# Swapped halves of x, another order of one block's loads and transposes, and two later steps in block 2

## The chip, the cores and the metric

The kernel runs on one core of a Trainium2 chip. The metric is the device time of one execution in microseconds (us), here the median over several runs; beside it stands one execution taken with the hardware profiler.

The profile knows these engines: PE (TensorE matrix multiplications), PEld (its weight loads, which overlap with PE), DVE (VectorE), ACT (ScalarE), POOL (GpSimd) and SP (SyncE, which here only issues DMAs). Each engine works through its own instruction list strictly in the written order and waits at an instruction until what it needs is there. A row "SPq" is an instruction that issues a DMA from SP's list; the transfer itself is over later.

## The reference

Attention inside chunks of 64 rows, then a feed-forward layer with a squared ReLU. With 8 batches, 8 heads, 576 rows and 64 values per head:

```
scores = q_c @ k_c.T / sqrt(64)                 # per chunk of 64 rows
attn   = exp(scores - max) / (sum + 1e-9)
x      = (attn @ v_c) as [4608, 512]            # heads side by side
h      = relu(x @ w_in)                         # w_in: 512 x 2048
out    = (h * h) @ w_out                        # w_out: 2048 x 512
```

## The kernel before, in words

**Groups and blocks.** The 4608 rows are cut into 18 groups of 256 rows (four chunks). Two groups make a block, so there are nine blocks, 0 to 8; block j holds the groups 2j and 2j+1. Groups 14 and 15 (block 7) collect the last chunk of each batch; all other groups are "whole", four chunks in a row of one batch.

**The steps of a group.** Its q, k and v are loaded (`qk_pieces`, `v_pieces`; SP issues them). `cast_qk` (step C) turns q and k into bf16, `transpose_qk_dma` (step TD) transposes them with one DMA on SP's list. `scores` (SC) makes the scores on PE and their exponentials on ACT. `values` (AV, or in two halves AV0 and AV1) multiplies with v on PE and divides on DVE (`out_of_x`, lines 431 and 432), which gives x. `transpose_x` (XT) brings x into the transposed tile xT of its block: up to group 11 on PE (line 526) with a copy on ACT (line 531), from group 12 on as one DMA on SP's list (line 521). A DMA that waits for x or for a cast holds up everything behind it in SP's list.

**PSUM banks of attention.** Up to block 3, SC, each half of AV and each XT take the next of two alternating banks (`att_bank`); a step can start to write only when the one two before it has been read out, by DVE for AV and by ACT for SC and XT.

**The feed-forward of blocks 0 to 3.** `ffn_in` has 16 slots, one for each 128 columns of w_in; PE multiplies, ACT makes the ReLU (line 576) and DVE or ACT the square (lines 583, 581). From block 1 on the second product runs as seven products of half size (`ffn_out`), whose operands are sums of pieces of g, made on DVE (`g_sum`, line 599 with outputs in `w_st`). In block 2 the sums are issued in slots 14 and 15, slots 16 to 18 issue nothing on PE, and the products begin with slot 19. A plan by slot says after which slot the steps of the next block's attention are issued.

**The feed-forward of blocks 4 to 8.** Here the first product is split as well. A block is cut into four steps of w_in (Q, 20 in all), each with seven small products (`quad_step`: A1, B2, A6, C5, A7, C3, A4). Four of them take sums of quarters of xT that DVE makes in `x_sums`: e1, e2, e3 and e4. A quarter is `xs(j, dh, th)`, where `th` says which half of the block's rows it is. In order of use:

```
(e1, xs(j, 0, 1), xs(j, 1, 1), ALU.subtract),
(e2, e1, xs(j, 0, 0), ALU.add),
(e3, e2, xs(j, 1, 0), ALU.subtract),
(e4, xs(j, 0, 1), xs(j, 0, 0), ALU.add)
```

So e1, with which A1 opens a block, and B2, which follows, read only the half `th` = 1; A6 waits for e2, C5 for e3, and these read half 0 too. The steps A7, C3 and A4 of one Q are issued between A1, B2 and A6 of the next, and the seven products of the block before (`ffn_out`) stand between them.

**The order of the work.** The order on every engine is written out by hand: `run` goes through the ticks, one tick for a Q, four slots each, 16 slots to a block; a plan tells which attention steps, loads, casts, transposes and sums are issued in which slot, half slots included. During block j the attention of block j+1 runs and q, k and v of block j+2 are loaded. All loads, TD, and XT from group 12 on are in SP's one list in that order. Output tiles are stored by DMAs of POOL, which also makes some squares and the casts (those of groups 8 and 9 are made by ACT).

Of the kernel before, what the change touches and what calls it, by code (L numbers as in the profile page):

```python
# [144 lines left out]
def kernel(  # L145
# [22 lines left out]
    blocks = [[g, g + 1] for g in range(0, n_grp, 2)]  # L168
    n_blk = len(blocks)
# [7 lines left out]
    def is_whole(g):  # L177
        return chunks[g][0][0] == chunks[g][3][0]
# [5 lines left out]
    QUADS = 4  # L184
# [101 lines left out]
    for g in range(n_grp):  # L286
        if is_whole(g):
# [3 lines left out]
            b, s = chunks[g][0]  # L291
# [23 lines left out]
    def go(pieces):  # L315
        for f in pieces:
            f()
# [21 lines left out]
    state = {}  # L339
    banks = {}  # L340

    def x_tile(j):
        if j not in xTs:
            xTs[j] = att_pool.tile([128, BT // 128, n_dt, 128], BF16, name="xT", bufs=2)
        return xTs[j]

    def att_bank():
        if "out" in banks:
            return ps_att.tile([128, 1024], FP32, name="ps_att")
        state["att"] = state.get("att", 0) + 1  # L350
        if state["att"] % 2:
            return ps_att.tile([128, 1024], FP32, name="ps_att")
        return ps_att2.tile([128, 1024], FP32, name="ps_att2")
# [162 lines left out]

    def transpose_x(g):
        x = state.pop(("x", g))
        dst = x_tile(g // 2)[:, g % 2 * 2:g % 2 * 2 + 2].rearrange("p t h q -> p (t h) q")
        if g >= FIRST_DMA_X:  # L520
            nc.sync.dma_start_transpose(out=dst, in_=x.rearrange("p t h a d -> p (t h a d)"))
            return
        psb = att_bank().bitcast(BF16)[:, 0:1024].rearrange("p (b q) -> p b q", q=128)
        for t in range(2):
            for hp in range(n_hp):
                nc.tensor.transpose(  # L526
                    out=psb[:, t * n_hp + hp, :],
                    in_=x[:, t, hp].rearrange("p a d -> p (a d)"),
                    identity=ident)
        copy = nc.vector.tensor_copy if g == blocks[1][0] else nc.scalar.copy  # L530
        copy(out=dst, in_=psb)  # L531
# [5 lines left out]
    for j in range(n_blk):  # L537
        if j < QUADS:
            at = {(th, fh, h): 4 * th + 2 * fh + h
                  for th in range(2) for fh in range(2) for h in range(2)}  # L540
        else:
# [6 lines left out]
            at = {(*key, 0): s for key, s in zip(keys, old)}  # L548
# [164 lines left out]
    def ffn_out(j):  # L713
# [62 lines left out]
            return kept_sb[state["kept"] % 2]  # L776

        def store(dma, o_sb, half, col, t=None):
            g = blocks[j][half]
            b, s0 = chunks[g][0]  # L780
            t0 = b * S + s0
            if not is_whole(g):

                for p in range(2):
                    dma.dma_start(
                        out=out.rearrange("(b s) d -> s b d", s=S)[
                            s0:s0 + CH, b + p:b + 4:2, col:col + HD],
                        in_=o_sb[p * CH:(p + 1) * CH].rearrange("p (t d) -> p t d", d=HD))
            elif t is None:
                dma.dma_start(  # L790
                    out=out[t0:t0 + GT, col:col + HD].rearrange("(t p) d -> p t d", p=128),
                    in_=o_sb.rearrange("p (t d) -> p t d", d=HD))
            else:
                dma.dma_start(
                    out=out[t0 + t * 128:t0 + (t + 1) * 128, col:col + HD],
                    in_=o_sb[:, t * HD:(t + 1) * HD])
# [112 lines left out]
    SC, AV, XT = scores, values, transpose_x  # L909
    TD = transpose_qk_dma  # L910
# [67 lines left out]
    for j in range(QUADS):  # L978
        grps, nxt, far = blocks[j], blocks[j + 1], blocks[j + 2]
        plan = {}  # L980

        def at(slot, f, *x):
            plan.setdefault(slot, []).append((f, x))

        if j == 0:
            loads, go_slots = pieces(far), range(17)
            at(28, summed(b11_p_b21, b11, b21))
            for slot, f in ((24, TA), (27, SC), (29, AV), (31, XT)):
                at(slot, f, nxt[0])
            at(31, TQ, nxt[1])  # L990
            at(31, summed(b22_m_b21, b22, b21, ALU.subtract))
            phases = [first_ffn_in, ffn_out_by_ft(0)]
        elif j == 1:
            loads, go_slots = itertools.chain(*map(qk_pieces, far)), range(26, 48)
            for slot, f in ((1, TK), (4, SC), (7, AV), (12, XT)):
                at(slot, f, grps[1])
            for i, g in enumerate(nxt):
                for slot, f in ((16 + 4 * i, C), (21 + 4 * i, TD), (36 + i, SC), (38 + 2 * i, AV),
                                (41 + 2 * i, XT)):
                    at(slot, f, g)  # L1000
            for i, g in enumerate(far):
                at(36 + 4 * i, C, g)
                at(42 + 3 * i, TD, g)
            at(2, summed(b12_p_b21, b12, b21))
            at(12, summed(b11_m_b12, b11, b12, ALU.subtract))
            at(20, summed(b12_p_b22, b12, b22))
            out_j = ffn_out(1)
            for i in (20, 27, 29, 31):
                at(i, lambda: next(out_j)())
            phases = [ffn_in(1, [(0, 256, FT_ORDER), (256, 256, FT_ORDER)]), out_j]  # L1010
        else:
            out_j = ffn_out(j)
            for i in (14, 15):
                at(i, lambda: next(out_j)())
            phases = [ffn_in(j, [(0, BT, range(n_ft))])]
            if j == 2:
                loads, go_slots = itertools.chain(*map(v_pieces, nxt), pieces(far)), [
                    *range(16), *range(27, 36)]
                slots = {SC: (6, 9), AV: (11, 14), XT: (14, 17), C: (21, 26), TD: (25, 29)}
                for f in (C, TD):  # L1020
                    for i, g in enumerate(far):
                        at(slots[f][i], f, g)
                phases.append(out_j)
            else:
                loads, go_slots = pieces(far), range(11)
                for f, slots in ((C, (11, 13)), (TD, (13, 15))):
                    for i, g in enumerate(far):
                        at(slots[i], f, g)
                slots = {SC: (2, 4), AV: (7, 10), XT: (13, 15)}
            for f in (SC, AV, XT):  # L1030
                for i, g in enumerate(nxt):
                    at(slots[f][i], f, g)
            if j == 2:
                for i, f in enumerate((summed(a21_p_a22, a21, a22),
                                       summed(a12_m_a21, a12, a21, ALU.subtract),
                                       summed(a11_p_a21, a11, a21))):
                    at(1 + 2 * i, f)
        slot = 0
        for phase in phases:
            for _ in phase:  # L1040
                if slot in go_slots:
                    for f in loads:
                        f()
                        break
                for f, x in plan.get(slot, []):
                    f(*x)
                slot += 1
        assert all(x < slot for x in plan), (j, slot, sorted(plan))
        if j < QUADS - 1:
            go(loads)  # L1050
# [19 lines left out]
    for j in range(QUADS, n_blk):  # L1070
        if j == QUADS:
            n = 14 - LEAD
            slots = [1 + 19 * i // n for i in range(n)]
            assert len(slots) == n
        else:
            slots = [s for s in range(4, 20) if s % 16 not in NO_OUT]
# [20 lines left out]
        if j + 1 < n_blk:  # L1097
            S0, V0, V1, X0 = ((1.5, 3.5), (4.5, 7.5), (6, 9.5), (8.5, 11.5)) if j == QUADS else (
                (0.5, 7), (2, 8), (3.5, 9.5), (3.5, 10)) if is_whole(blocks[j + 1][0]) else (
                (3.5, 9), (5, 10), (7, 11.5), (11.5, 12))  # L1100
            for i, g in enumerate(blocks[j + 1]):
                at(j, S0[i], SC, g)
                at(j, V0[i], AV0, g)
                at(j, V1[i], AV1, g)
                at(j, X0[i], XT, g)
            if j + 2 == n_blk:
                at(j, 22, check_sums)
                at(j, 25.5, count_bad)
            for i, s in enumerate((13.5, 15, 17.5, 18)):
                at(j, s, x_sums, j + 1, i)  # L1110
# [3 lines left out]
            assert next(loads, None) is None  # L1114
        if j + 2 < n_blk:
            more = pieces(blocks[j + 2])
            for s in range(0, 16):
                at(j, s, load, 1 if is_whole(blocks[j + 2][0]) else 2, more)
            for i in range(2):
                at(j, (9, 13)[i], C, blocks[j + 2][i])  # L1120
                at(j, (12, 13.5)[i], TD, blocks[j + 2][i])
    tail = ffn_out(n_blk - 1)
    at(n_blk, 3, lambda: next(tail)())

# [63 lines left out]
```

## Time and profile before

| | |
|---|---|
| median of 3 runs | 288.05 us (287.52 to 288.37) |
| the profiled execution | 287.81 us, of which the profile's span is 286.0 us |
| PE busy | 269.3 us, 94% of the span |
| DVE, ACT, POOL busy | 70%, 58%, 32% |
| DMA bytes | 55.61 MB, mean 194 GB/s |

The profiled execution lies 0.24 us under the median. Rows of the timeline give the start in us from the span's start, how long, engine, line, operation, output and input tiles, and the count; a bracket at the end is the idle time of the engine just before, and what ended it. Equal instructions next to each other are merged into one row. The tile `qk_st` holds the staged q and k, but in the second half of the kernel also the sums e1 to e4 and some pieces of g. The weight sums live in `w_st`, `w_out_sum` and `qk_st`.

### The profile page before, as it was taken

What the parts mean: (1) busy time and instruction counts of PE and PEld (TensorE: products, weight loads), DVE (VectorE), ACT (ScalarE), POOL (GpSimd) and SP (SyncE); (2) the same over time, 40 slices, a digit from 0 to 9 for tenths busy, and PEclk for the clock granted to TensorE, in tenths of its full rate; (3) what the DMA queues carried; (4) which work ended last, traced back from release to release, by engine and by line L of the source; (5) the groups of instructions that cost most, each with busy time, mean ns of one, the idle gap of its engine ahead of it and who ended that gap; (6) DMA issues with size and microseconds to landing.
All of it is one profiled execution on the core that took longest, in us unless ns stands there. A gap on an engine that the chain in (4) does not pass through costs nothing.

```text
span 286.0 us, 7983 instructions
## 1 busy us (share of the span) xinstructions
PE 269.3 (94%) x3291; PEld 205.6 (72%) x3291; DVE 199.1 (70%) x367; ACT 166.0 (58%) x296; POOL 91.8 (32%) x123
## 2 busy tenths in 40 slices
PE   2999999999999799999999999999969999999994
PEld 2774445788764478447879888888847888888783
DVE  1276515999537671599989997789638877994841
ACT  1537614894458664875778666575626654766320
POOL 2047733240450001141245344522612322431612
PEclk9999999999999999999999999999988999999998
DMA  7999999989999976999998997798997320220313
GB/s 220 241 312 388 389 307 274 328 196 168 300 190 232 239 149 145 279 239 189 227 236 175 218 218 182 145 220 193 267 175 170 76 70 6 87 62 7 94 55 112
DMA packets 135480, 55.61 MB, mean 194 GB/s; under 512 B 104272, under 2 KB 131152, under 8 KB 135440
## 3 DMA queue, kind: packets, MB, share of 16 engines
q1 hardware_dynamic: 132432, 45.76, 69.3%
q0 software_dynamic: 2864, 9.18, 9.8%
q8 instruction: 27, 0.44, 0.6%
q10 hardware_dynamic: 144, 0.13, 0.1%
q14 instruction: 13, 0.11, 0.1%
HBM read 36.70 MB, written 9.44 MB: 161 GB/s over the span
## 4 chain that ended last, share of the span: by engine, by line
PE 81%; DVE 7%; DMA 4%; ACT 3%; SPq 3%; issue 1%; ACTq 0%
PE ps_ffn L642 20%; PE ps_out L761 19%; PE ps_ffn L565 15%; PE ps_ffn L761 13%; PE ps_ffn L877 5%; DMA qk_st<-in_k_dram 3%; DVE gT L583 2%; PE ps_att L470 2%; PE ps_att L497 2%; DVE x L432 2%; SPq L279 2%; PE ps_ffn L422 1%; PE ps_att L526 1%; DVE w_st L599 1%; PE ps_ffn L389 1%
## 5 line engine op out<-in xcount | busy, mean ns | idle before, releaser
L565 PE MATMUL ps_ffn<-xT,w_in_bf 128*128 128x512 bf16 (+1 forms) x328 | 58.7, 333 | 0.4 <-DVE xT L531 0.2
L761 PEld LDWEIGHTS <-w_st 128*128 128x128 bf16 x512 | 49.1, 98 | 8.3 <-DVE w_st L599 1.6
L650 DVE CUSTOM_DVE_ANT_0 relu<-ps_ffn,w_st 128x512 f32<-128x512 f32 x60 | 39.4, 684 | 14.5 <-PE ps_ffn L642 13.1
L583 DVE TENSOR_TENSOR gT<-relu 128x256 bf16<-128x256 bf16 (+2 forms) x69 | 33.7, 516 | 20.3 <-ACT relu L576 19.9
L576 ACT ACTIVATE relu<-ps_ffn 128x256 bf16<-128x256 f32 (+2 forms) x82 | 39.9, 503 | 11.7 <-PE ps_ffn L565 10.1
L565 PEld LDWEIGHTS <-w_in_bf 128*128 128x128 bf16 x328 | 30.9, 98 | 21.6 <-DVE xT L531 0.4
L642 PE MATMUL ps_ffn<-qk_st,w_in_bf 128*128 128x256 bf16 x240 | 35.3, 273 | 2.8 <-DVE qk_st L599 2.8
L790 POOL DMA_DIRECT2D out_dram<-o_sb x27 | 19.8, 733 | 53.1 <-DVE o_sb L599 52.0
L642 PEld LDWEIGHTS <-w_in_bf 128*128 128x128 bf16 x320 | 30.8, 98 | 7.3 <-DVE qk_st L599 3.1
L761 PE MATMUL ps_out<-w_out_bf,w_st 128*128 128x256 bf16 x240 | 31.0, 273 | 0.4 <-DVE w_st L599 0.4
L761 PEld LDWEIGHTS <-gT 128*128 128x128 bf16 x296 | 28.6, 98 | 3.4
L684 ACT ACTIVATE w_st<-ps_ffn 128x512 f32<-128x512 f32 x20 | 11.9, 597 | 25.8 <-PE ps_ffn L642 25.8
L481 ACT ACTIVATE e<-ps_att 128x1024 bf16<-128x1024 f32 x18 | 18.4, 1024 | 13.4 <-PE ps_att L470 13.4
L432 DVE TENSOR_TENSOR x<-ps_att,recs 128x512 bf16<-128x512 f32 x36 | 24.9, 691 | 1.2
L642 PEld LDWEIGHTS <-qk_st 128*128 128x128 bf16 x240 | 22.8, 99 | 3.1
L642 PE MATMUL ps_ffn<-xT,qk_st 128*128 128x256 bf16 x160 | 24.4, 277 | 0.0
L661 POOL TENSOR_TENSOR qk_st<-relu 128x512 bf16<-128x512 f32 x10 | 10.3, 1034 | 41.7 <-DVE relu L650 41.7
L661 POOL TENSOR_TENSOR gT<-relu 128x512 bf16<-128x512 f32 x10 | 10.3, 1034 | 41.4 <-DVE relu L650 37.6
L761 PE MATMUL ps_ffn<-w_out_bf,w_st 128*128 128x256 bf16 x144 | 17.6, 273 | 0.3 <-DVE w_st L599 0.3
L659 ACT ACTIVATE gT<-relu 128x512 bf16<-128x512 f32 x28 | 17.7, 633 | 0.0
L438 POOL CAST qkb<-qk_st 128x1024 bf16<-128x1024 f32 x12 | 12.6, 1048 | 15.0 <-DMA qk_st<-in_q_dram 15.0
L599 DVE TENSOR_TENSOR w_st<-gT,w_st 128x1024 bf16<-128x1024 bf16 x26 | 17.3, 700 | 0.0
(91 smaller groups left out, 430.8 us busy)
## 6 DMA issues: line engine op xcount, KB each, us to landing
qk_st<-in_q_dram SPq DMA_DIRECT2D x16, 512.0 KB, 5.4
out_dram<-o_sb POOLq DMA_DIRECT2D x31, 256.0 KB, 4.1
qk_st<-in_k_dram SPq DMA_DIRECT2D x24, 256.0 KB, 5.6
ve_sb<-in_v_dram SPq DMA_DIRECT2D x32, 128.0 KB, 4.0
w_st<-in_moe_w_in_dram SPq DMA_DIRECT2D x8, 512.0 KB, 6.5
w_st<-in_moe_w_out_dram SPq DMA_DIRECT2D x8, 512.0 KB, 5.5
vo_sb<-in_v_dram SPq DMA_DIRECT2D x24, 128.0 KB, 3.4
qk_st<-in_k_dram SPq DMA_DIRECT2D x4, 512.0 KB, 5.9
```

What stands on the lines that cost most here:

```text
L432: nc.vector.tensor_tensor(out=x, in0=o[:, :, :, 0:D], in1=rec.to_broadcast([128, 2, n, D]), op=ALU.mult)
L481: nc.scalar.activation(out=e_out, in_=s_in, func=AF.Exp, scale=scale)
L565: nc.tensor.matmul(out=h[:, 0:n], lhsT=w_in_bf[:, dt, ft * 128:(ft + 1) * 128], rhs=xT[:, c // 128:(c + n) // 128, dt, :], start=(dt == 0) ...
L576: nc.scalar.activation(out=rl[:, 0:n], in_=h[:, 0:n], func=AF.Relu)
L583: nc.vector.tensor_tensor(out=dst, in0=src, in1=src, op=ALU.mult)
L599: nc.vector.tensor_tensor(out=out, in0=in0, in1=in1, op=op)
L642: nc.tensor.matmul(out=bank[:, f * GT:(f + 1) * GT], lhsT=a[:, dt, ft * 128:(ft + 1) * 128], rhs=b[:, :, dt, :], start=(first and f == 0 a ...
L650: nc.vector._custom_dve(TENSOR_ADD_SAT, out=out, in0=in0, in1=in1, s0=BIG, s1=0.0)
L659: engine.activation(out=dst, in_=r, func=AF.Square)
L661: engine.tensor_tensor(out=dst, in0=r, in1=r, op=ALU.mult)
L761: nc.tensor.matmul(out=out_ps, lhsT=lhsT, rhs=b[:, i, :], start=(first and i == 0 and (last or t == 0)), stop=(i == HF - 1), skip_group_ch ...
L790: dma.dma_start(out=out[t0:t0 + GT, col:col + HD].rearrange("(t p) d -> p t d", p=128), in_=o_sb.rearrange("p (t d) -> p t d", d=HD))
```

## The change

Four edits, none of which adds or removes an instruction:

- **Halves.** From block 4 on the even group of a block goes into half 1 of xT and the odd group into half 0 (`half_of`); the stores find the group that belongs to a half accordingly.
- **Block 2's attention steps** (for block 3): AV of group 7 is issued in slot 15 and no longer in 14; XT of group 7 in slot 24 and no longer in 17.
- **XT of group 14** (during block 6): in slot 7.5 and no longer in 11.5.
- **Block 6's loads** (of block 8, groups 16 and 17): the six loads of q and k stay one per slot in slots 0 to 5. The nine loads of v move from slots 6 to 14 to slots 10 (two), 12.5 (three) and 14 to 15.5 (four). TD of group 16 goes from slot 12 to 9.5. XT of group 15 (slot 12) and TD of group 17 (13.5) stay.

In SP's list of block 6 the order after the six loads of q and k was: six loads of v, XT 14, XT 15, one load of v, TD 16, one load of v, TD 17, the last load of v. It becomes: XT 14, TD 16, two loads of v, XT 15, three loads of v, TD 17, four loads of v.

```diff
+    def half_of(g):
+        return g % 2 if g // 2 < QUADS else 1 - g % 2
...
     def transpose_x(g):
         x = state.pop(("x", g))
-        dst = x_tile(g // 2)[:, g % 2 * 2:g % 2 * 2 + 2].rearrange("p t h q -> p (t h) q")
+        n = 2 * half_of(g)
+        dst = x_tile(g // 2)[:, n:n + 2].rearrange("p t h q -> p (t h) q")
...
         def store(dma, o_sb, half, col, t=None):
-            g = blocks[j][half]
+            g, = (g for g in blocks[j] if half_of(g) == half)
...
             if j == 2:
-                slots = {SC: (6, 9), AV: (11, 14), XT: (14, 17), C: (21, 26), TD: (25, 29)}
+                slots = {SC: (6, 9), AV: (11, 15), XT: (14, 24), C: (21, 26), TD: (25, 29)}
...
-                (3.5, 9), (5, 10), (7, 11.5), (11.5, 12))
+                (3.5, 9), (5, 10), (7, 11.5), (7.5, 12))
...
             more = pieces(blocks[j + 2])
-            for s in range(0, 16):
-                at(j, s, load, 1 if is_whole(blocks[j + 2][0]) else 2, more)
+            if j == n_blk - 3:
+                for s, n in ((0, 1), (1, 1), (2, 1), (3, 1), (4, 1), (5, 1), (10, 2), (12.5, 3),
+                             (14, 1), (14.5, 1), (15, 1), (15.5, 1)):
+                    at(j, s, load, n, more)
+            else:
+                for s in range(0, 16):
+                    at(j, s, load, 1 if is_whole(blocks[j + 2][0]) else 2, more)
             for i in range(2):
                 at(j, (9, 13)[i], C, blocks[j + 2][i])
-                at(j, (12, 13.5)[i], TD, blocks[j + 2][i])
+                at(j, ((9.5, 13.5) if j == n_blk - 3 else (12, 13.5))[i], TD, blocks[j + 2][i])
```

## The prediction

> **What bounds the kernel now.** I read the page first, for the span, PE's share and the granted clock by slices; then PE's waits; then the timeline of each engine around the two long waits.
>
> ```profile
> span 286.0 us, 7983 instructions
> PEclk9999999999999999999999999999988999999998
> ```
>
> ```profile
> PE ps_ffn L642 <- DVE qk_st L599: 2.8, 1, 2.8
> PE ps_att L526 <- DVE x L432: 1.8, 1, 1.8
> ```
>
> ```profile
> 211.60:217.20 5.60, 5.57 (x64) 4.15 (x65) 4.14 (x8) 1.84 (x3) 2.45 (x3) 0.70 1.06 198
> 217.00:268.00 51.00, 51.00 (x546) 44.36 (x544) 39.93 (x75) 31.64 (x58) 13.52 (x16) 1.00 0.21 57
> ```
>
> PE is the bound: from 217 to 268 us it is busy all 51.00 us (first pair of a window row; the last three numbers are granted clock, DMA share, GB/s). What can be won lies in its two waits and in what follows them: right after the 2.8 us wait the mean clock is 0.70 for 5.6 us. 0.30 x 5.60 = 1.7 us of PE's speed are lost there, on top of the wait.
>
> **The opening of block 7.**
>
> ```profile
> 208.19 0.60 PE L761 MATMUL ps_out<-w_out_bf,qk_st 128*128 128x256 bf16 x4
> 211.63 0.61 PE L642 MATMUL ps_ffn<-qk_st,w_in_bf 128*128 128x256 bf16 x4 [2.84 <-DVE qk_st L599]
> ...
> 215.93 0.48 PE L470 MATMUL ps_att<-qkT 64*64 64x64 bf16 x32
> 216.34 0.61 PE L642 MATMUL ps_ffn<-qk_st,qk_st 128*128 128x256 bf16 x4
> ...
> 218.19 0.22 PE L497 MATMUL ps_att<-ve_sb,e 64*64 64x65 bf16 x2
> ...
> 221.88 0.49 PE L761 MATMUL ps_out<-w_out_bf,w_st 128*128 128x256 bf16 x3
> ```
>
> ```profile
> 181.76 0.60 PE L642 MATMUL ps_ffn<-qk_st,w_in_bf 128*128 128x256 bf16 x4
> ...
> 184.38 0.60 PE L642 MATMUL ps_ffn<-qk_st,qk_st 128*128 128x256 bf16 x4
> ```
>
> ```profile
> 211.14 0.43 DVE L599 TENSOR_TENSOR qk_st<-xT 128x512 bf16<-128x512 bf16 x1 [3.90 <-DMA xT<-x]
> ```
>
> The row at 211.63 is A1 of block 7. It waits for e1 (DVE at 211.14), which waits for the DMA that transposes group 15. The second fence is the same stretch one block earlier, without a wait: from A1 (181.76) to A6 (184.38) 2.62 us. In block 7 the scores of group 16 stand before A6 as well: 216.34 - 215.93 = 0.41. Six groups of four matmuls fill the 2.62, 0.44 each, so after 208.19 A1 could start at 208.63 and A6 at 208.63 + 2.62 + 0.41 = 211.66. It starts at 216.34: wait and slow clock together cost **4.68 us**.
>
> **What the edits do to it.** SP's list, POOL's cast, and when the transposes land:
>
> ```profile
> 198.48 1.89 SPq L279 DMA_DIRECT2D qk_st<-in_k_dram  x2
> 200.41 1.95 SPq L307 DMA_DIRECT2D ve_sb<-in_v_dram  x2
> ...
> 205.90 3.32 SPq L521 DMA_TRANSPOSE xT<-x  x2
> ...
> 209.96 2.91 SPq L447 DMA_TRANSPOSE qkT<-qkb  x1
> ```
>
> ```profile
> 186.09 4.43 SPq L447 DMA_TRANSPOSE qkT<-qkb  x1
> ```
>
> ```profile
> 200.54 1.04 POOL L441 CAST qkb<-qk_st 128x1024 bf16<-128x1024 f32 x1 [1.85 <-DMA qk_st<-in_k_dram]
> ```
>
> ```profile
> 194.81 0.69 DVE L432 TENSOR_TENSOR x<-ps_att,recs 128x512 bf16<-128x512 f32 x1
> ```
>
> ```profile
> 203.76 0.69 DVE L432 TENSOR_TENSOR x<-ps_att,recs 128x512 bf16<-128x512 f32 x1
> ```
>
> ```profile
> xT<-x SPq DMA_TRANSPOSE x1, 4.1
> ```
>
> ```profile
> xT<-x SPq DMA_TRANSPOSE x1, 3.1
> ```
>
> ```profile
> qkT<-qkb SPq DMA_TRANSPOSE x1, 4.6
> ```
>
> The x of group 14 is done at 195.50, that of group 15 at 204.45; their transposes are issued only from 205.90, behind six loads of v, and land 4.1 and 3.1 us after issue.
>
> - *XT 14 early:* its x is long there, so SP issues it when the q and k loads are out, at 200.41, for about 1.7 us (half of 3.32). It lands by 204.5 instead of 210.0. With the swap e1 needs only this group: DVE can make e1 when it comes to it, after 207.2, and A1 starts at 208.63. Without the swap e1 would still wait for group 15; without the early slot it would wait until 210.0. The two edits earn this together.
> - *TD 16 before XT 15:* the cast of k ends at 201.58, so SP doesn't stand; the issue takes 2.91 (4.43 where it took longest), to 205.0 (206.5). It lands 4.6 after issue, by 207; the scores of group 16 want it at 211.25.
> - *Two loads of v:* 1.95, to 206.9 (208.5). They are wanted by AV0 of group 16, 218.19 - 4.68 = 213.5 at the earliest. Of the three that now follow XT 15 this step needs two; issued by about 210 and landing some 4.6 later at worst they come close to it. I take no wait, the worst price being about 1 us.
> - *XT 15:* issued at 206.9 (208.5), it lands 3.1 to 4.1 later, at 210.0 to 211.0 (at worst 212.6). e2 takes 0.4 and A6 wants it at 211.66: nothing in the middle case, 1.4 us at worst.
> - *DVE behind e2:* e2 now stands waiting on DVE, and the ReLUs of A7 and C3 behind it wait too, up to the sum that opens the next product of `ffn_out`.
>
> ```profile
> 220.15 0.68 DVE L599 TENSOR_TENSOR w_st<-qk_st,gT 128x1024 bf16<-128x1024 bf16 x1
> ```
>
> ```profile
> 212.50:220.83 8.33, 8.33 (x111) 6.23 (x111) 6.22 (x11) 4.86 (x9) 2.45 (x3) 0.80 0.83 188
> ```
>
> DVE has 6.22 us of work between the end of e2 and the end of that sum. PE wants it at 221.88 - 4.68 = 217.2. With e2 done at 210.4 to 211.4 the sum ends at 216.6 to 217.6: between no wait and 0.4. I take 0.
>
> The same swap at the openings of blocks 4, 5, 6 and 8 costs and earns nothing: at block 6's PE starts A1 without idle time as it is (row 181.76), no other wait for these sums stands in PE's list, and the half that comes later is wanted later. The stores write other rows with the same DMAs. TD 17 and the last four loads of v are wanted 8 us or more later than block 7's opening.
>
> In sentences that the sum does without: the Trainium skill, "TensorE: Matmul & The Clock Gate", section "Why this matters for your kernels", allows PE idle gaps of up to about 3 us before the clock falls. The row says 2.84 us and the clock fell, so the trace goes further than the page; by the page the fall would have some other cause and the edits would earn only the wait, 2.99 us. By the same skill, "DMA: Bandwidth & Descriptors", section "Issuing engines are not separate DMA queues", the time to issue is usually small beside the transfer; the rows here (2.91 of 4.6 us) say that SP's list matters.
>
> **Block 2.**
>
> ```profile
> 98.53 0.62 PE L526 MATMUL ps_att<-ident,x 128*128 128x128 bf16 x8 [1.79 <-DVE x L432]
> ...
> 99.86 0.61 PE L526 MATMUL ps_att<-ident,x 128*128 128x128 bf16 x8
> 100.30 1.91 PE L761 MATMUL ps_ffn<-w_out_sum,gT 128*128 128x256 bf16 x16
> ...
> 104.63 1.91 PE L761 MATMUL ps_ffn<-w_out_sum,w_st 128*128 128x256 bf16 x16 [0.67 <-ACT kept L818]
> ```
>
> ```profile
> 97.07 0.63 ACT L581 ACTIVATE gT<-relu 128x512 bf16<-128x512 bf16 x1
> 99.19 1.01 ACT L531 COPY xT<-ps_att 128x1024 bf16<-128x1024 bf16 x1 [1.49 <-PE ps_att L526]
> ```
>
> ```profile
> 95.67 0.69 DVE L432 TENSOR_TENSOR x<-ps_att,recs 128x512 bf16<-128x512 f32 x1
> ...
> 97.55 0.20 DVE L431 RECIPROCAL recs<-ps_att 128x8 f32<-128x8 f32 x1
> ...
> 98.62 0.69 DVE L432 TENSOR_TENSOR x<-ps_att,recs 128x512 bf16<-128x512 f32 x1
> 100.74 0.42 DVE L583 TENSOR_TENSOR gT<-relu 128x512 bf16<-128x512 bf16 x1 [1.42 <-ACT relu L576]
> ...
> 105.42 0.68 DVE L599 TENSOR_TENSOR o_sb<-ps_ffn,kept 128x512 f32<-128x512 f32 x1
> ```
>
> XT 6 (98.53) waits 1.79 us for DVE to empty the bank of AV 7's first half. In the new order XT 6 comes before AV 7 and takes the bank of AV 6: it starts when x of group 6 is done, 95.67 + 0.69 = 96.36. XT and slot 15's matmuls take 99.86 - 98.53 = 1.33, to 97.7. Then AV 7: its second half needs the bank of XT 6, whose copy on ACT runs after the square of 97.07, from 97.70 to 98.71. So the products start at about 98.95 and not at 100.30: 1.35 earlier. But AV 7's four instructions on DVE now stand behind the seven sums. The square of slot 15 comes after its ReLU, which follows the copy: 99.25 for 100.74. From there to the end of the sums it is 105.42 - 100.74 = 4.68, to 103.93, and AV 7 takes 98.62 + 0.69 - 97.55 = 1.76: x of group 7 at 105.69. PE is through the third product at 98.95 + (104.63 - 100.30) + 1.75 = 105.03 (two products follow each other by 1.75 where no wait stands between them) and waits for it in slot 24, then needs 0.44 for XT 7: 106.18. Before, the third product ended at 104.63 + 1.75 = 106.38. **Gain 0.2 us.** If neither new wait came (98.71 - 97.9 and 105.7 - 105.03, 1.5 together) it would be 1.7; if the square came no earlier than 100.74, x would come at 107.2 and the loss would be 1.3. I take 0.2, from the chain of rows. The copy of XT 7 is wanted only by block 3's first slot, over 6 us later.
>
> **Sum.** 287.81 - 4.68 - 0.2 = 282.93 in terms of the profiled execution; the median is 0.24 higher: **283.2 us**.
>
> **Rivals.**
> - *The wait moves to e2 or behind it (0.15).* XT 15 lands at 212 to 213, or the sum behind e2 is late. For it: TD's 4.43 us row and the load of DVE; against it: DMA engines and SP are then free of six loads of v. A wait of 1 to 2.5 us, with the clock kept: 284.2 to 285.7.
> - *The clock falls all the same (0.06),* by the page's rule or because a shorter gap is enough: only 2.99 of the 4.68 is earned, 288.05 - 2.99 - 0.2 = 284.9.
> - *Nothing changes (0.04):* XT 14 lands no earlier because its DMA queues behind q and k, 288.
> - *Slower (0.11): SP stands at TD 16.* Everything behind it, XT 15 first, waits. If XT 15 lands at 214.2, A6 starts as late as before (214.65 plus the slow clock); from there each us is a us lost. It needs TD 16 to hold SP until 211, 4.5 us over its longest row. At 216 the time is 289.7.
>
> **How the numbers follow.** The forecast has 0.64: 282.2 to 284.0, from a gain of 1 in block 2 to waits of 0.8 in block 7. The range for 8 in 10 reaches into the first rivals: 282.0 to 286.6. Three runs tell about 0.3% (0.9 us) from no change. Faster 0.85 (the forecast and the first two rivals), same 0.04, slower 0.11.
>
> **What would show it.** Right: A1 of block 7 without idle time, clock 1.00 from 208 to 217, the XT of group 14 issued near 200.4 and landing by 205, e2 and not e1 as the sum that waits for xT. Block 2: XT 6 near 96.4, and waits of about 0.8 and 0.7 us at AV 7's second half and at XT 7. Wrong: a PE wait over 1 us at A6, at AV0 of group 16 or at the first product with the new sum; a half-speed stretch that stays.

## The result, and the profile after

| | before | after |
|---|---|---|
| median of 22 runs each | 287.66 us (285.15 to 289.08) | 285.96 us (282.88 to 288.08) |
| the profiled execution | 287.81 us, span 286.0 us | 286.53 us, span 284.8 us |
| mean granted clock in it | 0.991 | 1.000 |

The ratio is 0.9935 with an interval of 0.9906 to 0.9965: the change makes the kernel faster by 1.7 us. The forecast was 4.85 us (288.05 to 283.2). The direction is right, the size is about a third: 285.96 us lies above the forecast's 282.2 to 284.0, though inside the range for 8 in 10 (282.0 to 286.6). (The ratio leaves disturbed runs out, so it is not exactly the quotient of the two medians.)

From here on line numbers are those of the changed kernel, which are 4 or 5 higher: L526 is XT as a DMA, L451 TD, L604 the sums on DVE, L647 the products of the Qs, L766 those of `ffn_out`, L531 XT on PE, L536 its copy, L501 AV, L436 the division that gives x, L474 the scores, L655 a ReLU on DVE, L823 the copy to `kept`.

The page of the kernel after, its span and the granted clock by slices:

```profile
span 284.8 us, 7979 instructions
PEclk9999999999999999999999999999999999999999
```

The slow slice is gone. PE's waits in the kernel after (engine, tile and line; what was waited for; us in all, times, the longest):

```profile
PE ps_ffn L647 <- DVE qk_st L604: 2.5, 3, 1.2
PE ps_att L501 <- ACT xT L536: 0.7, 1, 0.7
PE ps_att L531 <- DVE x L436: 0.7, 2, 0.4
PE ps_ffn L766 <- ACT kept L823: 0.7, 1, 0.7
```

Of one wait of 2.8 us for a sum three have become, 2.5 us together. The 1.8 us at XT 6 are gone; of the other lines, the second is the wait that was forecast at AV 7's second half, the third holds one of 0.44 us in block 1 (group 3) and one of 0.26 us at XT 7, and the last stood before as well. The first line is where the forecast was missed; the timeline of PE at the opening of block 7 shows which steps wait:

```profile
208.59 0.60 PE L766 MATMUL ps_out<-w_out_bf,qk_st 128*128 128x256 bf16 x4
210.10 0.61 PE L647 MATMUL ps_ffn<-qk_st,w_in_bf 128*128 128x256 bf16 x4 [0.91 <-DVE qk_st L604]
...
212.83 0.45 PE L474 MATMUL ps_att<-qkT 64*64 64x64 bf16 x32
214.43 0.61 PE L647 MATMUL ps_ffn<-qk_st,qk_st 128*128 128x256 bf16 x4 [1.15 <-DVE qk_st L604]
...
217.15 0.60 PE L647 MATMUL ps_ffn<-qk_st,w_in_bf 128*128 128x256 bf16 x4 [0.40 <-DVE qk_st L604]
```

A1 waits 0.91 us, A6 1.15 us and C5 0.40 us. DVE's timeline names the sums they wait for:

```profile
209.62 0.43 DVE L604 TENSOR_TENSOR qk_st<-xT 128x512 bf16<-128x512 bf16 x1 [1.98 <-DMA xT<-x]
...
213.94 0.43 DVE L604 TENSOR_TENSOR qk_st<-qk_st,xT 128x512 bf16<-128x512 bf16 x1 [3.30 <-DMA xT<-x]
214.28 0.68 DVE L655 CUSTOM_DVE_ANT_0 relu<-ps_ffn,w_st 128x512 f32<-128x512 f32 x1
...
215.48 1.28 DVE L655 CUSTOM_DVE_ANT_0 relu<-ps_ffn,w_st 128x512 f32<-128x512 f32 x2
216.68 0.41 DVE L604 TENSOR_TENSOR qk_st<-qk_st,xT 128x512 bf16<-128x512 bf16 x1
```

e1 (209.62) and e2 (213.94) each wait for a transpose; e3 (216.68) only stands behind the work that e2 held up. So both transposes, XT 14 and XT 15, came late. SP's list of the kernel after shows when they were issued (start, how long SP was busy with it):

```profile
198.96 1.97 SPq L279 DMA_DIRECT2D qk_st<-in_k_dram  x2
201.09 2.22 SPq L526 DMA_TRANSPOSE xT<-x  x1
203.41 5.49 SPq L451 DMA_TRANSPOSE qkT<-qkb  x1
208.94 1.14 SPq L307 DMA_DIRECT2D ve_sb<-in_v_dram  x2
210.19 1.27 SPq L526 DMA_TRANSPOSE xT<-x  x1
```

And this is how long they took from issue to landing (the view of DMA issues for the stretches 202 to 203, 203.3 to 203.6 and 210 to 210.4 us; the first line is a store by POOL, the second XT 14, the third TD 16, the last XT 15):

```profile
out_dram<-o_sb POOLq DMA_DIRECT2D x1, 256.0 KB, 7.3
xT<-x SPq DMA_TRANSPOSE x1, 8.5
...
qkT<-qkb SPq DMA_TRANSPOSE x1, 7.7
...
xT<-x SPq DMA_TRANSPOSE x1, 3.7
```

XT 14 was issued at 201.09, nearly as forecast (200.41 there), but landed at 209.6, 8.5 us later. It landed at 210.0 in the kernel before: issued 4.8 us sooner, it came 0.4 us sooner. What A1 gained, it gained because with the swap it no longer needs XT 15, which landed at 211.1 in before. TD 16 held SP for 5.49 us, XT 15 went out only at 210.19 and landed at 213.9.

**What was won where, in the two profiled executions.** Their spans differ by 1.2 us, not by the 1.7 of the medians. Outside block 2 PE goes through the same list of work in both kernels (3291 weight loads in each), so the start of the same step in both traces can be compared: a row below is how much later (+) or earlier (-) it starts than before, and each step between rows is what that stretch cost or earned.

| PE's list up to | after minus before, us | step |
|---|---|---|
| start of block 0's work | +0.10 | |
| end of block 1 | +0.93 | +0.83: waits at x of group 3 above all, which the change does not touch |
| behind block 2 | +0.42 | -0.50 |
| last product before A1 of block 7 | +0.40 | |
| A1 | -1.52 | -1.92: the wait is shorter |
| scores of group 16 | -3.14 | -1.62: the clock stays at full speed |
| A6 | -1.77 | +1.37: the new wait for e2 |
| C5 and the rest | -1.32 | +0.45: the new wait for e3 |

The opening of block 7 thus earned 1.92 + 1.62 - 1.37 - 0.45 = 1.72 us where 4.68 was forecast, block 2 earned 0.50 where 0.2 was. (That 1.72 is also the difference of the medians is chance: with block 1's +0.83 the profiled execution is only 1.3 us ahead at the end.) The +0.83 differs from run to run in all kernels (0 to 0.8), so it says nothing of the change. The 0.91 and 1.15 us of the timeline are what PE sat idle at A1 and A6.

### The profile page after: what moved, and what is told of

Same layout as the page of the kernel before. It is cut to its first block, busy times and chain, and to the rows that moved or that the text cites. A ratio compares the mean times of both kernels' runs of the same rounds, so it can differ in the third digit from the quotient of the medians.

```text
span 284.8 us, 7979 instructions
## 1 busy us (share of the span) xinstructions
PE 268.3 (94%) x3288; PEld 204.9 (72%) x3291; DVE 200.2 (70%) x367; ACT 166.3 (58%) x296; POOL 92.7 (33%) x123
## 4 chain that ended last, share of the span: by engine, by line
PE 78%; DMA 8%; DVE 7%; ACT 3%; SPq 2%; issue 2%; DVEq 0%; ACTq 0%
PE ps_ffn L570 18%; PE ps_ffn L647 18%; PE ps_out L766 17%; PE ps_ffn L766 11%; PE ps_ffn L882 5%; DMA xT<-x 4%; DMA qk_st<-in_k_dram 3%; PE ps_att L474 2%; DVE w_st L604 2%; PE ps_att L501 2%; PE ps_ffn L426 1%; DVE gT L588 1%; ACT relu L581 1%; DVE x L436 1%; PE ps_ffn L393 1%
## 5 line engine op out<-in xcount | busy, mean ns | idle before, releaser
L766 PEld LDWEIGHTS <-w_st 128*128 128x128 bf16 x512 | 49.0, 98 | 8.3 <-DVE w_st L604 1.6
L655 DVE CUSTOM_DVE_ANT_0 relu<-ps_ffn,w_st 128x512 f32<-128x512 f32 x60 | 39.3, 684 | 12.7 <-PE ps_ffn L647 11.7
L647 PE MATMUL ps_ffn<-qk_st,w_in_bf 128*128 128x256 bf16 x240 | 35.3, 273 | 1.3 <-DVE qk_st L604 1.3
L647 PEld LDWEIGHTS <-w_in_bf 128*128 128x128 bf16 x320 | 30.6, 98 | 5.7 <-DVE qk_st L604 1.2
L766 PE MATMUL ps_out<-w_out_bf,w_st 128*128 128x256 bf16 x240 | 31.0, 273 | 0.4 <-DVE w_st L604 0.4
L766 PEld LDWEIGHTS <-gT 128*128 128x128 bf16 x296 | 28.5, 98 | 3.4
L436 DVE TENSOR_TENSOR x<-ps_att,recs 128x512 bf16<-128x512 f32 x36 | 24.9, 691 | 1.2
L647 PEld LDWEIGHTS <-qk_st 128*128 128x128 bf16 x240 | 22.6, 98 | 4.1 <-DVE qk_st L604 1.3
L647 PE MATMUL ps_ffn<-xT,qk_st 128*128 128x256 bf16 x160 | 23.9, 273 | 0.0
L442 POOL CAST qkb<-qk_st 128x1024 bf16<-128x1024 f32 x12 | 13.5, 1127 | 13.8 <-DMA qk_st<-in_q_dram 13.8
L766 PE MATMUL ps_ffn<-w_out_bf,w_st 128*128 128x256 bf16 x144 | 17.6, 273 | 0.3 <-DVE w_st L604 0.3
L604 DVE TENSOR_TENSOR w_st<-gT,w_st 128x1024 bf16<-128x1024 bf16 x26 | 16.9, 683 | 0.0
```

Of the source, the lines that this page charges most:

```text
L436: nc.vector.tensor_tensor(out=x, in0=o[:, :, :, 0:D], in1=rec.to_broadcast([128, 2, n, D]), op=ALU.mult)
L604: nc.vector.tensor_tensor(out=out, in0=in0, in1=in1, op=op)
L647: nc.tensor.matmul(out=bank[:, f * GT:(f + 1) * GT], lhsT=a[:, dt, ft * 128:(ft + 1) * 128], rhs=b[:, :, dt, :], start=(first and f == 0 a ...
L655: nc.vector._custom_dve(TENSOR_ADD_SAT, out=out, in0=in0, in1=in1, s0=BIG, s1=0.0)
L766: nc.tensor.matmul(out=out_ps, lhsT=lhsT, rhs=b[:, i, :], start=(first and i == 0 and (last or t == 0)), stop=(i == HF - 1), skip_group_ch ...
```

## The experiments

The open question: why did XT 14 take 8.5 us to land, and is that the whole reason? Three causes were to be told apart. **The queue:** XT 14 is issued right behind 1 MB of q and k loads, the last of which landed at 204.4 in the kernel after; its packets stand behind theirs. **TD 16:** it is issued right behind XT 14. **The store:** POOL issues a store of 256 KB at 202.05, whose packets share the DMA engines with the transposes. The window of 204.5 to 208.7 us in the kernel after (busy time of PE, PEld, DVE, ACT, POOL with counts; then clock, DMA share, GB/s):

```profile
204.50:208.70 4.20, 4.20 (x41) 3.75 (x39) 3.00 (x4) 2.46 (x5) 2.60 (x3) 1.00 1.25 117
```

The q and k loads are in, only transposes and the store are under way, there are always packets in flight (a packet counts whole where it starts, so the share can pass 1), and they move 117 GB/s. The packet records say why so little: most packets take what they take elsewhere (the store's of 4096 B about 0.17 us, the transposes' of 256 B 0.018 us), but 14 of the store's 64 take 1.67 to 2.29 us and two of a transpose 1.25. They are 16, as many as there are DMA engines, and for about 1.3 us nothing else moves. The same happens where no store runs: in the trace of the run below with the store later, 14 packets of a transpose take 1.38 to 1.41 us from 205.1 us on, one 1.27. The first row is the kernel after, the second that run:

```profile
206.10:207.30 1.20, 1.20 (x14) 1.07 (x12) 1.17 (x2) 0.69 (x2) 1.00 (x2) 1.00 0.06 9
```

```profile
205.20:206.40 1.20, 1.20 (x14) 1.08 (x12) 1.17 (x3) 0.00 (x0) 1.20 (x3) 1.00 0.12 6
```

So these standstills are no sign of the store. What it costs must be read from runs with and without it.

Where nothing else is said, an edit is made to the changed kernel, and times and ratios are against the kernel before on the same chip (medians there 288.00, 288.09 and 287.61 us).

**The same kernel again, as the scale for the others.** No edit.

> The changed kernel once more, on the same chip as its variants. All theories: 285 to 286.5 us, 0.4 to 0.9% under the kernel before. If the late landing of the transpose of group 14 is not of every execution, this profile may show it landing 4 us after issue, with A1 waiting for nothing.

Measured: 285.73 us, ratio 0.9948 (0.9901 to 0.9994). XT 14 was issued at 199.08 and landed at 207.1, 8.0 us later; TD 16 held SP for 5.13 us; XT 15 was issued at 207.77 and landed at 211.6. A1 did not wait this time, A6 waited 1.29 us and C5 0.40 us, and the opening earned 2.66 us (block 2 0.50 again). The long landing is no accident of one execution; whether it reaches A1 is a matter of a microsecond, and XT 15 is late in both.

**The store later.** The store of block 5's first output tile goes 26 steps behind its product and not 8 (`defer` takes the number as an argument here; the line that uses it is shown).

```diff
-            defer(lambda: store(nc.gpsimd, o, half, col))
+            defer(lambda: store(nc.gpsimd, o, half, col), 26 if (j, half, col) == (5, 0, 0) else 8)
```

> The changed kernel, with one store of POOL (block 5's first output tile, issued at 202.05 in the changed kernel's trace, 1 us behind the issue of the transpose of group 14) held back to the next two stores, at about 216. Theory 1 (that store and the two DMA transposes hold each other up on the DMA engines): the transpose of group 14 lands within 5 us of its issue, by about 206, SP is through with the transpose of q and k of group 16 in about 3 us (5.49 in the changed kernel), PE opens block 7 without idle time, and the time falls by 1.5 to 3 us against the changed kernel, to about 283.5. Theory 2 (the transpose of q and k of group 16, right behind, holds group 14's up): it lands 7 to 9 us after issue as before, the time stays at 286. Theory 3 (the loads of q and k ahead of it are what takes the time): the same as theory 2.

Measured: 284.87 us, ratio 0.9907 (0.9869 to 0.9945). SP's list, and the time from issue to landing of XT 14 and, in the second row, of TD 16:

```profile
200.54 2.39 SPq L526 DMA_TRANSPOSE xT<-x  x1
203.03 3.29 SPq L451 DMA_TRANSPOSE qkT<-qkb  x1
206.37 1.22 SPq L307 DMA_DIRECT2D ve_sb<-in_v_dram  x2
207.68 1.32 SPq L526 DMA_TRANSPOSE xT<-x  x1
```

```profile
xT<-x SPq DMA_TRANSPOSE x1, 6.2
...
qkT<-qkb SPq DMA_TRANSPOSE x1, 6.3
```

XT 14 lands at 206.8, in time for A1; SP is free 2.2 us sooner at TD 16 (3.29 for 5.49 us), and neither A1 nor A6 waits. The opening earned 4.18 us. The 0.4 us left are C5's wait for e3. So the store looks like a part of the cause; all profiles together are taken up below. It is not all of it: 6.2 us is still 2.1 us more than the 4.1 us that the forecast took, and more than the 5 that the first theory allowed. By time alone this kernel can't be told from the unchanged one (0.9 us, where that theory expected 1.5 to 3), their intervals overlap; the landing and the waits tell them apart.

**The store earlier.** `2 if ... else 8` in the same place.

> The same store six steps earlier instead, at about 198, ahead of the casts of group 16 and beside the loads of q and k. Theory 1: the store is over or nearly over before the transpose of group 14 starts; that lands within 5 us of its issue, by about 206, and the time falls by 1 to 3 us against the changed kernel; the loads of q and k may come up to 1 us later. Theories 2 and 3: landing 7 to 9 us after issue, time as the changed kernel or up to 1 us longer.

Measured: 284.86 us, ratio 0.9923 (0.9884 to 0.9962). XT 14 was issued at 201.60 and landed at 207.6, 6.0 us later. But the store now ran beside the q and k loads, and the last of these landed only at 205.8; XT 15 landed at 212.6, and PE waited 1.9 us in two waits, 1.5 us the longest. The opening earned 2.44 us. Out of XT 14's way, the store was in that of the loads ahead of it.

**XT 14 ahead of group 17's loads.** The three loads of q and k of group 17 go from slots 3 to 5 to slots 8 to 9, behind XT 14 at 7.5.

```diff
-                for s, n in ((0, 1), (1, 1), (2, 1), (3, 1), (4, 1), (5, 1), (10, 2), (12.5, 3),
+                for s, n in ((0, 1), (1, 1), (2, 1), (8, 1), (8.5, 1), (9, 1), (10, 2), (12.5, 3),
```

> The changed kernel, with the transpose of group 14 issued ahead of the three loads (1 MB) of q and k of group 17 and no longer behind them; what stands ahead of group 15's transpose stays the same, in another order. If a transpose waits its turn in the queue behind the loads issued before it: group 14's is issued near 196 (its x is done at 195.9 in the changed kernel) and lands by 203, A1 waits for nothing, and group 15's lands as late as it did, at 211 to 214, so that A6 still waits 0.5 to 1.5 us; 0.3 to 1 us faster than the changed kernel. If the transpose itself takes its 8 us beside any loads: it lands at 204 or later all the same.

Measured: 284.87 us, ratio 0.9916 (0.9880 to 0.9951). SP's list, and XT 14's time from issue to landing:

```profile
194.67 1.94 SPq L279 DMA_DIRECT2D qk_st<-in_k_dram  x2
196.78 3.58 SPq L526 DMA_TRANSPOSE xT<-x  x1
...
203.15 4.80 SPq L451 DMA_TRANSPOSE qkT<-qkb  x1
...
209.22 1.24 SPq L526 DMA_TRANSPOSE xT<-x  x1
```

```profile
xT<-x SPq DMA_TRANSPOSE x1, 5.6
```

The last load that now stands ahead of XT 14 landed at 201.3, and XT 14 landed at 202.4, 1.1 us behind it. So it comes behind the loads ahead of it in SP's queue, here by about as much as in the kernel before (0.9 us); the store began only at 202.45, when XT 14 had landed. A1 no longer waits. But TD 16, now itself behind 1 MB of loads and beside the store, holds SP for 4.80 us; XT 15 lands at 212.8, and A6 waits 1.06 us, C5 0.40 us. The opening earned 2.90 us.

**TD 16 behind XT 15.** Its slot goes from 9.5 back to 12.

```diff
-                at(j, ((9.5, 13.5) if j == n_blk - 3 else (12, 13.5))[i], TD, blocks[j + 2][i])
+                at(j, ((12, 13.5) if j == n_blk - 3 else (12, 13.5))[i], TD, blocks[j + 2][i])
```

> The changed kernel, with the transpose of q and k of group 16 back in slot 12, behind the transpose of group 15 and two loads of v. Theory 1: the store still meets the transpose of group 14, which lands 6 to 9 us after its issue; group 15's comes right behind it, by about 211 and not 213.85; PE still waits at A1, hardly at A6: 0.5 to 1.5 us faster than the changed kernel. Theory 2: group 14's lands within 5 us of its issue, group 15's by 209, no wait for the sums; about 2 us faster, unless the scores of group 16 come late. Theory 3: both as late as in the changed kernel or nearly.

> The changed kernel with the transpose of q and k of group 16 behind that of group 15, once more, on the same chip as the next two. About 284.6 us; no wait for the sums e1 to e3, group 15's transpose landing by 210.5.

Measured, twice: 284.57 us, ratio 0.9906 (0.9864 to 0.9947), and 283.84 us, ratio 0.9889 (0.9846 to 0.9933). SP's list of the first, and the times from issue to landing of XT 14 and XT 15:

```profile
201.53 2.19 SPq L526 DMA_TRANSPOSE xT<-x  x1
203.76 1.42 SPq L307 DMA_DIRECT2D ve_sb<-in_v_dram  x2
205.47 2.54 SPq L526 DMA_TRANSPOSE xT<-x  x1
208.10 1.82 SPq L451 DMA_TRANSPOSE qkT<-qkb  x1
```

```profile
xT<-x SPq DMA_TRANSPOSE x1, 6.8
...
xT<-x SPq DMA_TRANSPOSE x1, 4.6
```

XT 15 goes out at 205.47 and lands at 210.0; in the second run 204.46 and 210.5, although XT 14 took 8.3 us there. (So it isn't TD 16 right behind it that makes XT 14 late.) Waits for sums are gone but for 0.19 us at A1 in the second. The new place has a price of its own: the scores of group 16 now wait for TD 16, 0.15 us in the first run and 0.98 us in the second, as this row of the second run's timeline of PE shows:

```profile
212.74 0.44 PE L474 MATMUL ps_att<-qkT 64*64 64x64 bf16 x32 [0.98 <-DMA qkT<-qkb]
```

The openings earned 4.40 and 3.22 us, more than either profile of the unchanged kernel.

**The two together.** Store later and TD 16 behind XT 15.

> Both at once: the transpose of q and k of group 16 behind that of group 15, and the store of POOL held back. If each of the two earns its gain on its own (1 us each) the time is about 283.8; if they earn the same thing, the opening of block 7 without waits, it is that of the transpose edit alone, 284.5. Group 14's transpose lands 5 to 6 us after issue and group 15's by 209.5.

Measured: 283.29 us, ratio 0.9869 (0.9828 to 0.9911). XT 14 landed at 206.9, XT 15 at 209.4, no wait for a sum, 0.35 us for TD 16; the opening earned 4.20 us. The forecast's ratio for the change, 283.2 / 288.05 = 0.983, lies just inside this interval.

**Parts of the change alone.** First the swap without the new order and without block 2's edits (`if False` in place of `if j == n_blk - 3` for the loads, XT 14 at 11.5, TD 16 at 12, AV and XT of block 2 in their old slots).

> The kernel before, with the halves swapped from block 4 on and nothing else. The transpose of group 14 landed at 210.0 there and that of group 15 at 211.1, so A1 opens block 7 about 1.1 us earlier: idle time of 1.7 us for 2.8 and, if the clock then stays up, 1.7 us more. Expected 0.8 to 2.8 us faster than the kernel before. If the swap alone does nothing, the rest of the gain is in the order.

Measured: 286.81 us, ratio 0.9970 (0.9935 to 1.0004). In its profile A1 waited 2.85 us and the opening earned 0.04 us. But this profile is the slowest of the 12 runs (289.10 us; the others 285.76 to 288.03): in block 5 the scores waited 1.16 us for a qkT, which no other profile shows, and both transposes were issued 1.1 to 1.2 us later against PE's work than in before, so that the 1.1 us between XT 14 and XT 15 was lost again. What the swap alone earns in the other runs it doesn't show.

Then the new order and early XT 14 without the swap and without block 2's edits (`half_of` returns `g % 2`).

> The changed kernel without the swap and without the edit of block 2: only the new order in SP's list of block 6. e1 then waits for group 15, whose transpose landed at 213.85 in the changed kernel and at 211.1 before. If that landing is what the new order makes, A1 waits until 214.3 and the clock falls: 2 to 3 us slower than the kernel before. If the prediction's landing (210 to 211) were right in most executions: the same as before or up to 1 us faster.

Measured: 290.85 us, ratio 1.0070 (1.0023 to 1.0118). XT 15 landed at 212.5 and A1, which without the swap needs it, waited 3.70 us. The new order alone is slower than the kernel before: it puts TD 16 ahead of XT 15, and A1 pays for it. The order earns only with the swap, as forecast.

Both, without block 2's edits:

> The changed kernel without the edit of block 2. If the parts add up, it is 0.2 to 0.6 us slower than the changed kernel, about 1.2 us faster than the kernel before.

Measured: 286.25 us, ratio 0.9965 (0.9924 to 1.0006), by time not told from no change, nor from the swap alone (0.9970): that the swap, too, earns only with the order is not shown. In its profile XT 14 landed at 208.3, XT 15 at 212.7, PE waited 0.6 us for sums, and the opening earned 3.75 us. Since the unchanged kernel earned 1.72 and 2.66 us in two profiles, the opening's gain moves by a us or two from run to run with the landing times.

Block 2's edits alone, on the kernel before (slots `AV: (11, 15), XT: (14, 24)`):

> The kernel before with only block 2's two steps moved. Predicted 0.2 us faster; the changed kernel's trace shows 0.5 us between the same instructions of PE. Expected 0.2 to 0.6 us faster, waits of about 0.7 us each at the second half of AV of group 7 and up to 0.7 at its transpose. A rival: the place shifts and with it what meets the later transposes, so that the sum moves by something else.

Measured: 286.51 us, ratio 0.9988 (0.9941 to 1.0034). Block 2 itself earned 0.51 us, as in each profile with these two slots (0.50 to 0.52), too little for the runs to tell. Its opening of block 7 waits as long as before, but the clock did not fall; that is taken up below.

**The best of it.** Store later, TD 16 behind XT 15, and in block 2 AV of group 7 in slot 20 and its XT in slot 27, behind the sums on DVE that the forecast saw them wait for:

```diff
-                slots = {SC: (6, 9), AV: (11, 15), XT: (14, 24), C: (21, 26), TD: (25, 29)}
+                slots = {SC: (6, 9), AV: (11, 20), XT: (14, 27), C: (21, 26), TD: (25, 29)}
```

> The same, and in block 2 AV of group 7 in slot 20 and XT of group 7 in slot 27. AV then finds its second bank read out by ACT long before (0.7 us of wait in slot 15), and XT comes two products later, when its x is done (0.4 us of wait in slot 24): 0.7 to 1.1 us less between the same instructions of PE. If a copy on ACT that comes later makes another wait, less.

Measured: 282.83 us (6 runs), ratio 0.9848 (0.9802 to 0.9893), about 4.4 us under the kernel before by the ratio; its interval lies below that of the kernel after too (0.9906 to 0.9965). Page, and PE's longest waits (the first line is that for the first load of q, at the start):

```profile
span 280.4 us, 7978 instructions
```

```profile
PE ps_ffn L393 <- DMA qk_st<-in_q_dram: 4.8, 1, 4.8
PE ps_ffn L766 <- ACT kept L823: 0.7, 1, 0.7
```

No wait for a sum from xT is left, nor one at AV 7 or XT 7. Block 2 earned 1.68 us, the opening of block 7 4.62 us, of which 0.4 us was given back later at the scores of group 17 (TD 17).

## Why the prediction was wrong in size and right in direction

- **What bounds the kernel: right.** PE stayed busy for 94% of the span, and what was won and lost were waits of PE and the clock behind one.
- **The size of the term, 4.68 us: right,** for an execution in which the clock falls, as in the profile it was read from (the last section says how many don't). Where both transposes land in time the opening earns 4.20, 4.40 and 4.62 us. The parts agree: in the best kernel A1 starts 3.01 us earlier (wait 2.99 forecast), and the full clock earned 1.62 us in the kernel after (1.69).
- **"XT 14 early ... It lands by 204.5": the step that failed.** The issue time was right to 0.7 us, the landing wrong by 5.1 us. The forecast took the 4.1 us of the row in which XT 14 was issued in before, as if it went with the transpose wherever it is issued. It isn't the queue ahead that made the difference: in before the last load ahead of XT 14 landed 3.2 us after XT 14's issue (209.10), in the kernel after 3.3 us (204.39). Behind that load XT 14 landed 0.9 us later in before, 5.2 in the kernel after. One part is POOL's store, which the forecast did not cost at all though its issue at 201.53 was in the trace; in before it landed at 206.87, ahead of the last of those loads, and in the new place XT 14 runs beside it. Without it XT 14 took 6.0 to 6.6 us (four profiles), beside it 6.8 to 8.5 (six, XT 14 in the same place), 1.3 us more in the mean, and in each of the six XT 14 landed 0.2 to 0.3 us behind the store. The other part stays without the store, 1.9 to 2.8 us behind the last load for 0.9 in before; part of it may be the standstill shown in the experiments (1.4 us in the run with the store later), and the rest, with what makes the standstill, stays open. In the profiled execution this left A1 a wait of 0.91 us (its start gained 1.92 us where the best kernel's gained 3.01); in the second profile of the kernel after it just did not.
- **"TD 16 before XT 15 ... SP doesn't stand": failed with it.** The cast was there in time, as said, but the issue held SP for 5.49 us, where 2.91 was taken and 4.43 was the worst. XT 15 went out at 210.19 for 206.9, and landed at 213.9, beyond the 212.6 that stood as the worst. Price: 1.37 us at A6. With TD 16 behind XT 15 this wait is gone in both runs, while XT 14 still takes long (6.8 and 8.3 us). Its issue, 203.41 to 208.90, spans the standstill of the DMA engines; at this place it took 3.99 to 5.49 us beside the store (four profiles) and 3.29 and 3.91 without. Beyond that the runs don't say what sets it. (A smaller slip: XT 14's issue was taken as half of a row of two, 1.7 us; it is the longer of the two, 1.97 us in before and 2.22 at the new place.)
- **DVE behind e2: in part.** The forecast looked at the sum for `ffn_out` (between 0 and 0.4, 0 taken). What was late is e3, and C5 waited 0.40 us for it in both profiles of the kernel after, and with the store later too, where A6 did not wait.
- **The loads of v and the other openings: right.** No wait of PE stands at any of them. That the stores change nothing was right for those that the swap concerns; the one of block 5 is the cost above.
- **The clock: right.** It stayed at 1.00, with waits of up to 1.15 us. The rival "the clock falls all the same" did not come in any profile with both edits. Single runs may have had such a fall: one of the 34 of the kernel after shows a mean clock of 0.991, and three of the 12 without block 2's edits 0.991 to 0.993.
- **Block 2: right in its chain, small.** XT 6 and AV 7 show the order of waits that was described:

```profile
97.11 0.64 PE L531 MATMUL ps_att<-ident,x 128*128 128x128 bf16 x8
...
99.58 0.22 PE L501 MATMUL ps_att<-ve_sb,e 64*64 64x65 bf16 x2 [0.71 <-ACT xT L536]
...
106.56 0.40 PE L531 MATMUL ps_att<-ident,x 128*128 128x128 bf16 x4 [0.26 <-DVE x L436]
```

  XT 6 waits for nothing but its x (97.11 less the 0.83 us of block 1's delay is 96.3), AV 7's second half 0.71 us (0.8 forecast), XT 7 0.26 us (0.7). The gain was 0.50 us for 0.2 forecast, more by about what XT 7's wait was shorter. "If neither new wait came ... 1.7": the best kernel took both away and earned 1.68.
- **The rivals.** What came is nearest to "the wait moves to e2 or behind it, with the clock kept" (284.2 to 285.7, chance 0.15), for the reason given there, XT 15 at 212 to 213; but it needed A1's own wait beside it to reach 285.96. "Slower: SP stands at TD 16" was the same mechanism at a higher price: XT 15 at 213.9 lay just short of the 214.2 from which it decides, and without the swap it did decide (ratio 1.0070). "Nothing changes: XT 14 lands no earlier" (chance 0.04) was nearly right in XT 14's landing (209.6 for 210.0), though not by the queue behind q and k; its 288 us did not follow, since A1 no longer needed XT 15.

## What to carry to other kernels

A DMA that is issued earlier does not land earlier by as much (here 0.4 us for 4.8). Its landing has to be built up at the new place: when the last transfer ahead of it in its queue lands, and what other engines' queues move from then on. The issue-to-landing time of a row at the old place holds neither. When several transfers wait on one issuing engine, the one with the earliest consumer goes first, and a large one ahead of it costs its whole issue time under load. A stall that is cut into waits of about 1 us kept the clock here, which was worth 1.6 us beside a wait of 3. And a kernel whose profile has a fall of the clock in it should be profiled more than once before the fall is counted as a gain.

## What the runs showed of the hardware that was not expected

**A transpose beside a store, and standstills.** XT 14 took 8.5 and 8.0 us beside POOL's store and 6.2 without; the store took 7.3 us from issue to landing beside XT 14 and TD 16, and 4.2 us where it ran 11 us later. The Trainium skill, "DMA: Bandwidth & Descriptors", section "Issuing engines are not separate DMA queues", says that DMAs started by different engines run on the same 16 DMA engines and interleave. The traces agree: packets of the store and of the transposes start in the same quarters of a microsecond. Beyond that, every profile has stretches of about 0.5 to 2.3 us in which some 16 packets or more are in flight and almost nothing moves (9 and 6 GB/s in the two rows of the experiments), most of them 2 to 4 us behind the issue of a transpose, with a store and without. What in the DMA engines does this the traces don't show.

**Behind its queue by 1 us.** Where neither the store nor a standstill of more than 1 us lay over it, a transpose of x in block 6 landed about 1 us behind the last transfer ahead of it in SP's list: XT 15 in before and in the kernel after 1.1 us, XT 14 in before 0.9 and ahead of group 17's loads 1.1.

**When the clock falls.** The change of the clock in before's trace, at 212.64 us, lies a whole number of 3.413 us steps (59) behind its rise at 11.25 us, and its slow stretch is one such step long. Windows on this grid, first before, from the step in which PE idles to the next:

```profile
209.22:212.64 3.42, 1.01 (x10) 0.92 (x11) 1.35 (x3) 0.37 (x1) 0.00 (x0) 1.00 1.03 204
212.64:216.05 3.41, 3.41 (x25) 2.20 (x26) 2.09 (x4) 0.75 (x2) 2.44 (x3) 0.50 0.97 191
```

the swap alone:

```profile
209.32:212.73 3.41, 0.75 (x7) 0.43 (x5) 0.28 (x1) 0.51 (x1) 0.00 (x0) 1.00 1.17 185
212.73:216.15 3.42, 3.22 (x16) 2.31 (x17) 1.86 (x4) 1.11 (x2) 0.39 (x1) 0.50 0.99 198
```

block 2's edits alone:

```profile
206.08:209.49 3.41, 2.48 (x23) 1.97 (x21) 0.93 (x1) 2.10 (x4) 0.39 (x1) 1.00 1.06 175
209.49:212.91 3.42, 1.50 (x14) 1.36 (x15) 1.64 (x4) 0.85 (x2) 0.00 (x0) 1.00 1.05 204
```

All three have the same wait, 2.84 or 2.85 us. In the first two PE was busy for 1.01 and 0.75 us of one step (idle for 2.41 and 2.66), and the next step ran at half speed. In the third the wait straddles an edge, 0.93 and 1.92 us idle, and the clock stayed. The end of the best kernel's profile narrows it further: PE, through with its work, was idle for 2.05 us of one step, and the clock fell at the next edge.

```profile
274.84:278.25 3.41, 1.36 (x13) 0.97 (x10) 0.50 (x2) 0.37 (x1) 0.72 (x1) 1.00 0.67 229
278.25:280.40 2.15, 0.00 (x0) 0.00 (x0) 0.00 (x0) 0.00 (x0) 0.00 (x0) 0.50 0.00 0
```

In all 14 profiles every fall, those at the end included, lies a whole number of these steps behind the rise, and after the rise every step with 2.05 us idle or more is followed by a fall, and none with 1.92 or less. So it is the idle time inside one step of a fixed grid that decided. The rise came anywhere between 9.8 and 12.4 us, so where the grid lies against the kernel's work differs from execution to execution. The Trainium skill, "TensorE: Matmul & The Clock Gate", section "What's actually happening", describes a free-running window of 3413 ns; these traces agree with it. The kernel before therefore is a mixture: of its 34 runs on one chip 11 had a mean clock of 0.997 or more (all but one of them 285.1 to 286.5 us), the others 0.985 to 0.994 (287.0 to 290.1 us). In another 35 runs there the two kinds overlap in time (12 of 284.9 to 289.8 us, the others 286.1 to 290.4), so the clock isn't all that differs. A single profile of before with a fall in it, as the forecast's was, shows 1.6 us that not every execution loses.
